# Gated linear attention beside a mixture of experts on one core: another order of the attention's operations, its result copied out a step earlier, 11 groups in place of 12 beside the first unit

## The chip, the cores and the metric

The kernel runs on one core of a Trainium2 chip. The metric is the device time of one execution in microseconds (us), as a median of three runs. TensorE is called PE, VectorE DVE, ScalarE ACT, GpSimd POOL, and SyncE, which only issues transfers here, SP.

## The reference, cut to what matters

A gated linear attention with 4 x 8 heads, 768 tokens and head size 48 gives x, 3072 rows of 384. A mixture of four experts (384 to 1024 to 384, all experts for every row, weighted) and one gated layer (384 to 2048 to 384) follow.

```python
for t in range(S):                                   # attention, for each head
    state = alpha[t][:, None] * state + outer(k[t], v[t])
    y[t] = q[t] @ state
x = y in rows of 384
p = domain_probs / (domain_probs.sum(-1) + 1e-9)
for e in range(4):
    out += p[:, e] * (relu(x @ w1[e]) @ w2[e])
h = out @ w_in
result = (h * clip(h + 3, 0, 6) / 6) @ w_out
```

## The kernel before, in words

**Attention.** The 3072 tokens are twelve units of 256, numbered n = 0 to 11, three for each batch entry. A unit is 7 *groups*, numbered g = 7n + k. Three tables of names give for each k what is emitted: `GROUP[k]` (mostly PE products), `BETWEEN[k]` (copies on ACT, products on DVE) and `CHUNK[k]`, called the *rest* of the group, which is emitted one step later. A name with `-` belongs to the unit before, with `+` to the unit after. The names that matter here:

- `T_tp`, `T_k`, `T_q` are PE transposes of decays, keys and queries, copied out of PSUM by ACT (`tl`, `kt`, `qt`, lines 313 and 334). `tls` multiplies decays on DVE (L342).
- `Sc0` to `Sc3` copy halves of `kt` and `qt` to `kc` and `qc` on ACT (L352). `Su0` to `Su3` then multiply `kt` and `qt` by decays in place on DVE (L362). `C0` to `C3` multiply `kc` by `qc` on PE (L374), `M0` and `M2` mask the result on DVE (L386), `K` turns the keys back (L400, copied by ACT at L408).
- `U` are the state sums on PE (L419), `Z` carries the state through them on DVE (L442, L448), `Y`, `L0` to `L3` and `ST` (the state products, L494) add up the unit's result in PSUM.
- `A` copies that result to SBUF on ACT (L506) and moves it with six transfers into x (L518). `XS` splits x into a high part `xh` (ACT, L802) and a low part `xl` (DVE, L803) and stores x (L805).
- `p0` to `p3`, `r0` to `r2`, `u0`, `u1`, `kk`, `kq`, `tp` prepare the next unit on DVE (L190 to L247). `y0` to `y5` are the value operations of the unit on DVE (L253 to L280).

**Experts.** Each product of the experts is made of three fp32r products: high by high, low by high, high by low. One *step* is a first layer `mm1` of nine products (L829), ACT's ReLU to `hh` (L837), DVE's low part `hl` (L840), and then the second layer `mm2` (L891) of the step before. After `mm1` and `hl` the rest of an earlier group is emitted, after `mm2` a group. Seven of the sixteen 256-column slices of expert weights stay in SBUF while the attention runs, so a block of rows takes 14 steps. Unit 0 and unit 1 are taken alone, with 256 columns (periods 0 and 1); from then on a block is 512 columns and two units. After six such periods the attention is over, and the rest of the experts and the last layer follow. In periods 0 and 1 the product of `mm1` goes to two PSUM tiles by turns; with 512 columns there is one, so the next `mm1` waits until DVE has read the last one for `hl`.

In period 0 the weights, too, are split in a high part (ACT, L779) and a low part (DVE, L781). The probabilities are normalised by four DVE operations (L639 to L643).

**Order.** PE, ACT, DVE and SP run in the order in which the code emits; POOL's is left to a scheduler. The list `ends` says up to which group each period goes: 12 groups (7 to 18) beside the first unit, then 14 in each period. Before period 0 stands a prologue, which runs unit 0 alone, with PE kept busy by idle products (L986).

Of the kernel before, what the change touches and what calls it, by code (L numbers as in the profile page):

```python
# [10 lines left out]
F32 = mybir.dt.float32  # L11
# [7 lines left out]
P = 128  # L19


class Attention:
# [23 lines left out]
    H = 7  # L46

    GROUP = (
        "T_tp -L2 -L3 T_k", "-ST T_q", "C0", "C1", "C2", "C3 K", "U Y L0 L1",
    )  # L50
    BETWEEN = (
        "-X tls", "Sc0 Su0", "Sc1 Su1", "Sc2 M0 Su2", "Sc3 Su3", "M2", "Z0 Z1 Z2 Z3",
    )
    CHUNK = (
        "y0 y1 y2 y3 y4 y5", "-A +p0 +r0", "+p1 +p2 +r1", "-XS +u0", "+u1 +cp +kk +kq", "+tp +p3 +r2", "",
    )

    def __init__(self, ctx, tc, q, k, v, alpha, psum_pool, psum_tag, place, split):
# [232 lines left out]
    def tree(self, n):  # L291
# [53 lines left out]
        def halves(z, l, x):  # L345
            return z.rearrange("p j r (b x w) -> p (j r b) x w", x=2, w=self.W[l])[:, :, x, :]

        def Sc(l):

            for z, out, x, nm in ((s["kt"], s["kc"], 0, "kc"), (s["qt"], s["qc"], 1, "qc")):  # L350
                c = self.wk.tile([P, NP * 2, 64], F32, tag=nm, name=f"{nm}{l}_{n}")
                nc.scalar.copy(c.rearrange("p x (b w) -> p (x b) w", w=self.W[l]), halves(z, l, x))  # L352
                out[l] = c

        def Su(l):

# [146 lines left out]
        def A():  # L503
            ys = wk("ys", [P, NP, U])
            for j in range(2):
                nc.scalar.copy(ys[:, :, P * j : P * j + P], s["py"][j])  # L506
            x = self.place(n)
            parts = (
                (x[0:48, 0:3], ys[0:48, 0:3]),
                (x[48:96, 0:3], ys[64:112, 0:3]),  # L510
                (x[96:128, 0], ys[0:32, 3]),
                (x[96:112, 1], ys[32:48, 3]),
                (x[112:128, 1], ys[64:80, 3]),
                (x[96:128, 2], ys[80:112, 3]),
            )
            for z, (dst, src) in enumerate(parts):
                eng = nc.scalar if n == 0 and z % 2 else nc.sync
                eng.dma_start(dst, src)  # L518

        d = dict(  # L520
            T_tp=T_tp, tls=tls, U=Ust, Y=Y, X=X, ST=ST, A=A,
            XS=lambda: self.split(n),
            T_k=lambda: T(self.kp, "kt"), T_q=lambda: T(self.qp, "qt"),
            M0=lambda: M(0), M2=lambda: M(2), K=K,
        )
        for l in range(4):
            d[f"Sc{l}"] = lambda l=l: Sc(l)
# [35 lines left out]
def tile_gla__then__moe__then__moe2(  # L563
# [458 lines left out]
    load_w(1, 3)  # L1022
    at.load(2, "qka")
    u("p3 r2", 1)
    emit_probs()
    load_p(0)
    load_p(1)


    g = at.H  # L1030
    ends = [3 * at.H - 2, 5 * at.H - 2]
    ends += [ends[1] + 2 * at.H * b for b in range(1, NBLK - 1)]

    todo = []
# [41 lines left out]
    for vi, vv in enumerate(visits):  # L1076
# [16 lines left out]
        for f in range(len(vv["steps"])):  # L1093
            for s_, fn in [x for x in todo if x[0] <= step]:
                todo.remove((s_, fn))
                fn()
            serve()
            low = mm1(vi, f)
            low()
            if rest:  # L1100
                at.rest(rest.pop(0))
            if late:
                next(dec, None)
            pend.append((vi, f))
            done = pend.pop(0) if len(pend) > 1 else None
            if done:
                mm2(*done)
            at_step += 1
            if period < len(ends):
                while g < begun + -(-(ends[period] - begun) * at_step // (2 * S0)):  # L1110
                    if rest:
                        at.rest(rest.pop(0))
                    at.group(g)
                    rest.append(g)
                    g += 1
                if at_step == 2 * S0 and rest:
                    at.rest(rest.pop(0))
            step += 1
            if done is None:
                continue  # L1120

            v2 = visits[done[0]]
            i, z = v2["steps"][done[1]]
            if v2["phase"] > 0 and done[1] == len(v2["steps"]) - 1:
                ended = step
            if done[1] == len(v2["steps"]) - 1 and done[0] + 2 < len(visits):
                after(3, lambda v_=done[0] + 2: load_p(v_))
            if v2["b"] == NBLK - 1 and z == 1:

                if v2["phase"] == 0 and i + S0 + SB < S1:  # L1130
                    get_w(i + S0 + SB)
                elif v2["phase"] == 1 and i - S0 < S2 - S1:
                    for _ in dec:
                        pass
                    get_w(i - S0 + S1)

            if i == (0, S0, S1)[v2["phase"]] + 2 and (v2["phase"] > 0 or v2["b"] == NBLK - 1):
                ph, nb = (v2["phase"], v2["b"] + 1) if v2["b"] + 1 < NBLK else (v2["phase"] + 1, 0)
                if ph <= 2:
                    n = 2 * nb + z  # L1140
                    loads.insert(z, (lambda ph=ph, n=n: load_x(ph, n), lambda ph=ph, n=n: split_x(ph, n)))
                    if ph == 1:
                        if z == 0:
                            load_acc(nb)
                        for e in range(1, EP):
                            loads.append((lambda e=e, n=n: load_acc1(e, n), lambda e=e, n=n: add_acc1(e, n)))
# [32 lines left out]
```

## Time and profile before

| | |
|---|---|
| median of three runs | 1385.18 us (1385.14 to 1385.52) |
| the profiled execution, its time | 1385.72 us |
| its span | 1383.7 us |
| PE busy | 1353.5 us, 98% |
| DVE busy | 843.4 us, 61% |
| ACT busy | 453.1 us, 33% |
| POOL busy | 83.2 us, 6% |
| period 0 | 42.1 to 101.8 us |
| period 1 | 101.8 to 164 us |

The shares are means over stages that differ. The page's 40 slices show DVE at 8 and 9 tenths for the first five slices (35 us each is one slice) and lower later, and PE at 9 from the sixth slice on. Two waits of PE in one list may be of the same cause; what an engine waits for at one place is read in the rows of that place.

### The profile page before, as it was taken

The numbers are of one execution on the slowest core, as the hardware profiler recorded it, in microseconds if no ns is written. First come the engines' busy times: TensorE is split into PE (matmuls) and PEld (weight loads), VectorE is DVE, ScalarE is ACT, GpSimd is POOL, SyncE is SP. The second block draws the span as 40 slices with busy tenths as digits, with TensorE's granted clock in tenths as the row PEclk, the third lists the DMA queues.
The fourth block names the chain that finished last, engine by engine and source line by source line (L and its number), as shares of the span: only waits on it lengthen the run. The fifth ranks groups of instructions, "written<-read, shape, count | busy, mean of one in ns | idle before, by whom it ended". The sixth has DMA issues, their size and how long they took to land.

```text
span 1383.7 us, 26396 instructions
## 1 busy us (share of the span) xinstructions
PE 1353.5 (98%) x10992; PEld 1130.3 (82%) x10992; DVE 843.4 (61%) x1524; ACT 453.1 (33%) x775; POOL 83.2 (6%) x125
## 2 busy tenths in 40 slices
PE   7789899999999999999999999999999999999998
PEld 7788788888888888888888888888888888888898
DVE  8998877777776368657576666645533333334332
ACT  3554444434443143111111111113333333333333
POOL 2000000000000001111112121100000000000000
PEclk9999999999999999999999999999999999999999
DMA  7655543444352276415142423223202020202010
GB/s 196 190 145 144 141 121 102 141 139 124 101 150 72 69 236 215 130 54 163 54 144 62 148 69 106 85 79 120 91 0 46 1 47 0 46 1 46 1 24 23
DMA packets 150279, 132.36 MB, mean 96 GB/s; under 512 B 65680, under 2 KB 130832, under 8 KB 150160
## 3 DMA queue, kind: packets, MB, share of 16 engines
q1 hardware_dynamic: 150016, 130.49, 32.7%
q8 instruction: 86, 1.41, 0.4%
q10 hardware_dynamic: 144, 0.20, 0.1%
q14 instruction: 33, 0.27, 0.1%
HBM read 95.99 MB, written 34.65 MB: 94 GB/s over the span
## 4 chain that ended last, share of the span: by engine, by line
PE 90%; DVE 6%; DMA 1%; ACT 1%; issue 1%; SPq 1%; POOL 0%; DVEq 0%; ACTq 0%; POOLq 0%
PE ph L829 42%; PE po L891 38%; PE po L893 2%; PE py L473 1%; PE py L494 1%; PE pa L374 1%; PE pu L419 1%; PE idle L986 1%; DVE asb L386 1%; DVE qt L362 1%; DVE kt L362 1%; PE pqt L322 0%; PE pkt L322 0%; DVE hl L840 0%; PE py L457 0%
## 5 line engine op out<-in xcount | busy, mean ns | idle before, releaser
L891 PE MATMUL po<-hl,w1h 128*128 128x512 f32 (+1 forms) x858 | 318.0, 380 | 10.1 <-DVE hl L840 10.0
L891 PE MATMUL po<-hh,w1h 128*128 128x512 f32 (+1 forms) x858 | 323.0, 379 | 0.0
L891 PE MATMUL po<-hh,w1l 128*128 128x512 f32 (+1 forms) x858 | 322.7, 379 | 0.0
L837 ACT ACTIVATE hh<-ph 128x512 fp32r<-128x512 f32 (+1 forms) x206 | 117.5, 571 | 500.8 <-PE ph L829 493.7
L840 DVE SCALAR_TENSOR_TENSOR hl<-ph,hh 128x512 fp32r<-128x512 f32 (+1 forms) x206 | 134.4, 652 | 240.6 <-ACT hh L837 240.6
L829 PE MATMUL ph<-xh,w0h 128*128 128x512 f32 (+1 forms) x906 | 255.3, 390 | 3.1 <-ACT xh L802 1.9
L829 PE MATMUL ph<-xh,w0l 128*128 128x512 f32 (+1 forms) x906 | 246.4, 380 | 0.0
L829 PE MATMUL ph<-xl,w0h 128*128 128x512 f32 (+1 forms) x906 | 245.8, 380 | 0.5 <-DVE xl L803 0.4
L829 PEld LDWEIGHTS ph<-xl,w0h 128*128 128x128 f32 x906 | 166.3, 188 | 33.8 <-DVE xl L803 1.1
L829 PEld LDWEIGHTS ph<-xh,w0l 128*128 128x128 f32 x906 | 166.6, 188 | 33.1
L891 PEld LDWEIGHTS po<-hl,w1h 128*128 128x128 f32 x858 | 157.8, 188 | 42.6 <-DVE hl L840 12.1
L829 PEld LDWEIGHTS ph<-xh,w0h 128*128 128x128 f32 x906 | 161.8, 188 | 35.9 <-ACT xh L802 2.2
L891 PEld LDWEIGHTS po<-hh,w1h 128*128 128x128 f32 x858 | 161.4, 188 | 30.8 <-ACT hh L853 0.5
L891 PEld LDWEIGHTS po<-hh,w1l 128*128 128x128 f32 x858 | 161.3, 188 | 30.1
L852 DVE SCALAR_TENSOR_TENSOR g<-g,ph 128x512 f32<-128x512 f32 (+1 forms) x97 | 66.2, 684 | 171.0 <-ACT g L848 171.0
L848 ACT ACTIVATE g<-ph,three 128x512 f32<-128x512 f32 (+1 forms) x97 | 66.2, 684 | 185.0 <-PE ph L829 185.0
L855 DVE SCALAR_TENSOR_TENSOR hl<-g,hh 128x512 fp32r<-128x512 f32 (+1 forms) x97 | 66.6, 687 | 66.6 <-ACT hh L853 66.6
L853 ACT ACTIVATE hh<-g 128x512 fp32r<-128x512 f32 (+1 forms) x97 | 60.9, 629 | 74.6 <-DVE g L852 74.6
L690 POOL TENSOR_TENSOR sq<-hc 128x256 f32<-128x256 f32 x48 | 34.5, 718 | 622.2 <-DVE hc L689 622.2
L934 DVE TENSOR_TENSOR t<-po,pb 128x512 f32<-128x512 f32 (+1 forms) x82 | 52.6, 655 | 0.0
L705 POOL TENSOR_TENSOR a<-a,hc 128x256 f32<-128x256 f32 x48 | 38.8, 808 | 184.6 <-DVE hc L704 184.6
L352 ACT COPY kc<-kt 128x512 f32<-128x512 f32 x48 | 30.3, 632 | 44.6 <-PE pa L374 31.7
(106 smaller groups left out, 1187.1 us busy)
## 6 DMA issues: line engine op xcount, KB each, us to landing
vl<-vd SPq DMA_DIRECT2D x96, 96.0 KB
rx<-x_d SPq DMA_DIRECT2D x24, 384.0 KB
pb<-p_d SPq DMA_DIRECT2D x28, 256.0 KB
raw<-in_moe_w_in_dram SPq DMA_DIRECT2D x24, 256.0 KB
raw<-in_moe_w_out_dram SPq DMA_DIRECT2D x24, 256.0 KB
acc_d<-t SPq DMA_DIRECT2D x20, 256.0 KB
rq<-in_q_dram SPq DMA_DIRECT2D x24, 192.0 KB
rk<-in_k_dram SPq DMA_DIRECT2D x24, 192.0 KB
```

The source lines that it names most:

```text
L352: nc.scalar.copy(c.rearrange("p x (b w) -> p (x b) w", w=self.W[l]), halves(z, l, x))
L690: nc.gpsimd.tensor_tensor(sq, hc, hc, op=mul)
L705: nc.gpsimd.tensor_tensor(a, a, hc, op=add)
L829: pe.matmul(ph[:, 0:n], w[:, j, fs], x[:, j, cs], start=(o == 0 and j == 0), stop=(o == 2 and j == KT - 1),)
L837: nc.scalar.activation(hh[:, 0:n], ph[:, 0:n], AF.Relu)
L840: nc.vector.scalar_tensor_tensor(hl[:, 0:n], ph[:, 0:n], 0.0, hh[:, 0:n].bitcast(F32), op0=ALU.max, op1=sub)
L848: nc.scalar.activation(g[:, c], ph[:, c], AF.Relu, bias=three)
L852: nc.vector.scalar_tensor_tensor(g[:, c], g[:, c], 6.0, ph[:, c], op0=ALU.min, op1=mul)
L853: nc.scalar.activation(hh[:, c], g[:, c], AF.Copy, scale=1.0 / 6.0)
L855: nc.vector.scalar_tensor_tensor(hl[:, c], g[:, c], 1.0 / 6.0, hh[:, c].bitcast(F32), op0=mul, op1=sub)
L891: pe.matmul(accs[vi][m][:, 0:n], w[:, z, ms], h[:, 0:n], **fl)
L934: nc.vector.tensor_tensor(t[:, 0:n], po[:, 0:n], pb, op=mul)
```

## The change

The result of a unit is copied out and moved right behind its state products (`-A` stands in `GROUP[1]`, no longer in the next step's rest). Its transfers go by turns to SP and POOL (for unit 0 to SP, ACT and POOL), where they all went to SP (for unit 0 to SP and ACT). The split of x stands first in the rest of k = 2, no longer in that of k = 3. `y4` moves from the rest of k = 0 to that of k = 1, and `y5` to that of k = 3. The copy `kc` of `Sc0` is made a group earlier, behind `tls`; `qc` stays. Period 0 takes 11 groups (7 to 17), with none added in its steps 3, 6 and 9; every later period begins and ends one group earlier than before. The probabilities are normalised behind the third step of period 0, no longer in the prologue, and their two loads are issued two steps behind that.

```diff
     GROUP = (
-        "T_tp -L2 -L3 T_k", "-ST T_q", "C0", "C1", "C2", "C3 K", "U Y L0 L1",
+        "T_tp -L2 -L3 T_k", "-ST -A T_q", "C0", "C1", "C2", "C3 K", "U Y L0 L1",
     )
     BETWEEN = (
-        "-X tls", "Sc0 Su0", "Sc1 Su1", "Sc2 M0 Su2", "Sc3 Su3", "M2", "Z0 Z1 Z2 Z3",
+        "-X tls Sk0", "Sq0 Su0", "Sc1 Su1", "Sc2 M0 Su2", "Sc3 Su3", "M2", "Z0 Z1 Z2 Z3",
     )
     CHUNK = (
-        "y0 y1 y2 y3 y4 y5", "-A +p0 +r0", "+p1 +p2 +r1", "-XS +u0", "+u1 +cp +kk +kq", "+tp +p3 +r2", "",
+        "y0 y1 y2 y3", "y4 +p0 +r0", "-XS +p1 +p2 +r1", "y5 +u0", "+u1 +cp +kk +kq", "+tp +p3 +r2", "",
     )
...
+        def S1(l, x):
+
+            z, out, nm = (("kt", "kc", "kc"), ("qt", "qc", "qc"))[x]
+            c = self.wk.tile([P, NP * 2, 64], F32, tag=nm, name=f"{nm}{l}_{n}")
+            nc.scalar.copy(c.rearrange("p x (b w) -> p (x b) w", w=self.W[l]), halves(s[z], l, x))
+            s[out][l] = c
...
             for z, (dst, src) in enumerate(parts):
-                eng = nc.scalar if n == 0 and z % 2 else nc.sync
-                eng.dma_start(dst, src)
+                engines = (nc.sync, nc.scalar, nc.gpsimd) if n == 0 else (nc.sync, nc.gpsimd)
+                engines[z % len(engines)].dma_start(dst, src)
...
-            M0=lambda: M(0), M2=lambda: M(2), K=K,
+            M0=lambda: M(0), M2=lambda: M(2), K=K, Sk0=lambda: S1(0, 0), Sq0=lambda: S1(0, 1),
...
     u("p3 r2", 1)
-    emit_probs()
-    load_p(0)
-    load_p(1)
...
-    ends = [3 * at.H - 2, 5 * at.H - 2]
+    ends = [3 * at.H - 3, 5 * at.H - 3]
+    first = [0, 1, 2, 2, 3, 4, 4, 5, 6, 6, 7, 8, 9, 10, 11]
...
-                while g < begun + -(-(ends[period] - begun) * at_step // (2 * S0)):
+                if period == 0 and at_step == 3:
+                    emit_probs()
+                    after(2, lambda: (load_p(0), load_p(1)))
+                while g < begun + (first[at_step] if period == 0 else (ends[period] - begun) * at_step // (2 * S0)):
```

Three places of the new order follow. A name ends with the unit, or with visit and step for `hh`, `hl` and the low weights; the last number counts tiles.

ACT in period 1, around the copy of unit 2's result (`ys`) and the queries of unit 3 (`qt`, `kc0`, `qc0`), before:

```order
L837 ACTIVATE hh_2_3_2009<-ph_2_3_1999 128x256
L334 COPY qt_3_2064<-pqt0_3_2065 128x8x16x4
L334 COPY qt_3_2064<-pqt1_3_2066 128x8x16x4
L352 COPY kc0_3_2085<-kt_3_1968 128x512
L352 COPY qc0_3_2087<-qt_3_2064 128x512
L837 ACTIVATE hh_2_4_2103<-ph_2_4_2093 128x256
L506 COPY ys_2_2107<-py0_2_1845 128x4x128
L506 COPY ys_2_2107<-py1_2_1846 128x4x128
```

and now:

```order
L352 COPY kc0_3_2022<-kt_3_1991 128x512
L842 ACTIVATE hh_2_4_2036<-ph_2_4_2026 128x256
L511 COPY ys_2_2088<-py0_2_1871 128x4x128
L511 COPY ys_2_2088<-py1_2_1872 128x4x128
L334 COPY qt_3_2098<-pqt0_3_2099 128x8x16x4
L334 COPY qt_3_2098<-pqt1_3_2100 128x8x16x4
L352 COPY qc0_3_2119<-qt_3_2098 128x512
L842 ACTIVATE hh_2_5_2133<-ph_2_5_2123 128x256
```

The copies of `ys` went ahead of those of `qt`, and `kc0` ahead of the ReLU of the step.

DVE in period 0, from the low weights behind unit 1's state (`Z`) to those behind unit 2's decays (`tl`), before:

```order
L781 TENSOR_TENSOR w0l_5_1279<-early_l_185,w0h_5_1278 128x768
L840 SCALAR_TENSOR_TENSOR hl_1_0_1293<-ph_1_0_1282,hh_1_0_1292 128x256
L934 TENSOR_TENSOR t_0_0_1302<-po_0_0_812,pb_0_729 128x256
L934 TENSOR_TENSOR t_0_1_1304<-po_0_0_812,pb_0_729 128x256
L934 TENSOR_TENSOR pb_0_729<-po_0_1_813,pb_0_729 128x256
L342 TENSOR_TENSOR tl1_2_1371<-tl0_2_1310 128x128
L342 TENSOR_TENSOR tl2_2_1373<-tl1_2_1371 128x64
L342 TENSOR_TENSOR tl3_2_1375<-tl2_2_1373 128x32
L342 TENSOR_TENSOR tl4_2_1377<-tl3_2_1375 128x16
L781 TENSOR_TENSOR w1l_5_1380<-early_h_184,w1h_5_1379 128x768
```

and now:

```order
L786 TENSOR_TENSOR w0l_6_1340<-early_h_184,w0h_6_1339 128x768
L845 SCALAR_TENSOR_TENSOR hl_1_2_1357<-ph_1_2_1346,hh_1_2_1356 128x256
L342 TENSOR_TENSOR tl1_2_1430<-tl0_2_1369 128x128
L342 TENSOR_TENSOR tl2_2_1432<-tl1_2_1430 128x64
L342 TENSOR_TENSOR tl3_2_1434<-tl2_2_1432 128x32
L342 TENSOR_TENSOR tl4_2_1436<-tl3_2_1434 128x16
L786 TENSOR_TENSOR w1l_6_1441<-early_l_185,w1h_6_1440 128x768
```

The three weighted sums of the first visit (`t`, `pb`), which stood here, now come ahead of `Z`; the place itself lies two steps later in the period.

DVE at the end of period 1, from the last `hl` with 256 columns to the first with 512, before:

```order
L840 SCALAR_TENSOR_TENSOR hl_3_5_2805<-ph_3_5_2794,hh_3_5_2804 128x256
L803 TENSOR_TENSOR xl_0_1_2234<-rx_0_3_2683,xh_0_1_2233 128x3x256
L200 TENSOR_TENSOR rq5_2366<-rq5_2366,ra5_2372 128x8x48
L362 TENSOR_TENSOR kt_4_2548<-kt_4_2548,tl3_4_2575 128x16x32
L362 TENSOR_TENSOR qt_4_2639<-qt_4_2639,tl3_4_2575 128x16x32
L203 TENSOR_TENSOR rk5_2369<-rk5_2369,ra5_2372 128x8x48
L205 TENSOR_TENSOR t1_5_2846<-ra5_2372 128x384
L216 TENSOR_TENSOR kp_111<-rk5_2369,t1_5_2846 128x2x2x48 x2
L216 TENSOR_TENSOR qp_110<-rq5_2366,t1_5_2846 128x2x2x48 x2
L840 SCALAR_TENSOR_TENSOR hl_4_0_2867<-ph_4_0_2856,hh_4_0_2866 128x512
```

and now:

```order
L845 SCALAR_TENSOR_TENSOR hl_3_5_2773<-ph_3_5_2762,hh_3_5_2772 128x256
L808 TENSOR_TENSOR xl_0_1_2202<-rx_0_3_2664,xh_0_1_2201 128x3x256
L193 TENSOR_TENSOR rq5_2394<-rq5_2394,ra5_2400 128x768
L197 TENSOR_TENSOR w1_5_2780<-rq5_2394,rk5_2397 128x384
L247 TENSOR_REDUCE dg1_5_2782<-w1_5_2780 128x8
L391 TENSOR_TENSOR asb0_4_2813<-pa00_4_2738,mask_123 128x512
L391 TENSOR_TENSOR asb0_4_2813<-pa01_4_2739,mask_123 128x512
L367 TENSOR_TENSOR kt_4_2574<-kt_4_2574,tl2_4_2599 128x32x16
L367 TENSOR_TENSOR qt_4_2671<-qt_4_2671,tl2_4_2599 128x32x16
L280 TENSOR_TENSOR y8_112<-y8_112,pr1_4_2625 128x2x2x48 x2
L200 TENSOR_TENSOR rq5_2394<-rq5_2394,ra5_2400 128x8x48
L845 SCALAR_TENSOR_TENSOR hl_4_0_2832<-ph_4_0_2821,hh_4_0_2831 128x512
```

`Su3` (the `kt` and `qt` with `tl3`) and the operations of `u1`, `kk` and `kq` (L203 to L216) left the stretch ahead of the first `hl` with 512 columns; the split of x now has more DVE work behind it.

## Rows read from the trace of the kernel before

**Rows 1.** Busy time by stretch: stretch, length, PE, PEld, DVE, ACT, POOL, clock, DMA, GB/s.

```profile
42.10:104.20 62.10, 51.04 (x834) 45.75 (x834) 59.55 (x115) 34.40 (x64) 0.00 (x0) 0.97 0.64 176
104.20:170.70 66.50, 58.53 (x1191) 52.95 (x1191) 57.63 (x123) 33.01 (x71) 0.00 (x0) 1.00 0.50 139
170.70:470.00 299.30, 299.27 (x4255) 242.03 (x4256) 214.84 (x408) 121.02 (x226) 0.00 (x0) 1.00 0.41 117
```

**Rows 2.** Waits of PE, 44 to 104 us: total, times, longest.

```profile
PE po L891 <- DVE hl L840: 8.4, 6, 2.4
```

**Rows 3.** Waits of DVE, 104 to 171 us.

```profile
DVE hl L840 <- ACT hh L837: 4.8, 2, 2.5
DVE kt L362 <- ACT kc L352: 1.3, 2, 0.8
```

**Rows 4.** DVE timeline, end of period 1: start, duration, operation, [idle before <- releaser].

```profile
166.55 0.68 DVE L362 TENSOR_TENSOR kt<-kt,tl 128x512 f32<-128x512 f32 x1
...
169.98 0.69 DVE L840 SCALAR_TENSOR_TENSOR hl<-ph,hh 128x512 fp32r<-128x512 f32 x1
```

**Rows 5.** PE timeline at the first step with 512 columns.

```profile
168.19 0.69 PE L374 MATMUL pa<-qc,kc 48*64 48x64 f32 x32
168.82 0.71 PE L400 MATMUL pk<-ident,kt 64*128 64x64 f32 x16
170.72 0.96 PE L829 MATMUL ph<-xh,w0h 128*128 128x512 f32 x3 [1.20 <-DVE hl L840]
```

**Rows 6.** DVE and ACT timeline, first two steps of period 0.

```profile
45.75 0.24 DVE L639 TENSOR_REDUCE probs<-probs 128x24 f32<-128x96 f32 x1
...
46.81 0.41 DVE L840 SCALAR_TENSOR_TENSOR hl<-ph,hh 128x256 fp32r<-128x256 f32 x1
...
48.04 0.95 DVE L781 TENSOR_TENSOR w1l<-early_h,w1h 128x768 fp32r<-128x768 f32 x1
...
46.52 0.86 ACT L779 CAST w1h<-early_h 128x768 fp32r<-128x768 f32 x1
```

**Rows 7.** DVE timeline behind unit 1's state, period 0.

```profile
81.04 0.74 DVE L934 TENSOR_TENSOR t<-po,pb 128x256 f32<-128x256 f32 x2
...
82.23 0.98 DVE L342 TENSOR_TENSOR tl<-tl 128x128 f32<-128x128 f32 x4
84.35 0.96 DVE L781 TENSOR_TENSOR w1l<-early_h,w1h 128x768 fp32r<-128x768 f32 x1 [1.15 <-ACT w1h L779]
```

**Rows 8.** DVE timeline, value operations of unit 3 and what follows.

```profile
121.98 0.56 DVE L274 TENSOR_TENSOR pr<-pr 128x384 f32<-128x384 f32 x1
122.58 0.63 DVE L280 TENSOR_TENSOR y<-y,pr 128x192 f32<-128x192 f32 x2
123.72 0.69 DVE L362 TENSOR_TENSOR kt<-kt,tl 128x512 f32<-128x512 f32 x1 [0.51 <-ACT kc L352]
```

**Rows 9.** ACT timeline at the same place.

```profile
123.02 0.67 ACT L352 COPY kc<-kt 128x512 f32<-128x512 f32 x1
123.56 0.62 ACT L352 COPY qc<-qt 128x512 f32<-128x512 f32 x1
...
124.35 1.09 ACT L506 COPY ys<-py 128x512 f32<-128x512 f32 x2
```

**Rows 10.** PE timeline, longest wait in period 0, and clock of the stretch behind it.

```profile
65.93 0.62 PE L891 MATMUL po<-hl,w1h 128*128 128x256 f32 x3 [2.42 <-DVE hl L840]
...
66.00:70.00 4.00, 4.00 (x58) 0.57 0.52 139
```

**Rows 11.** SP and ACT timelines: transfers of x and the split that waits.

```profile
36.98 2.25 SPq L518 DMA_DIRECT2D rx<-ys  x3
91.61 4.50 SPq L518 DMA_DIRECT2D rx<-ys  x6
...
41.21 0.83 ACT L802 CAST xh<-rx 128x768 fp32r<-128x768 f32 x1
97.64 0.83 ACT L802 CAST xh<-rx 128x768 fp32r<-128x768 f32 x1 [1.36 <-DMA rx<-ys]
```

More of the change, by code (lines that the diff above doesn't have):

```diff
@@ L346, in halves @@
             return z.rearrange("p j r (b x w) -> p (j r b) x w", x=2, w=self.W[l])[:, :, x, :]
+        def S1(l, x):
[3 more added lines that the diff above has]
+            s[out][l] = c
         def Sc(l):
[L350 to L353, printed above, removed]
+            for x in range(2):
+                S1(l, x)
         def Su(l):
```

## The prediction

> **What bounds the kernel now.** I read first the busy time by stretch [rows 1]. From 170.7 to 470 us PE is busy 299.27 of 299.30 us, so a change of order inside that stretch can only cost. What can be won lies ahead of it: PE stands 62.10 - 51.04 = 11.1 us in period 0 and 66.50 - 58.53 = 8.0 us in period 1. In period 0 DVE is busy 59.55 of 62.10 us, and the list of PE's waits shows why PE stands: 8.4 us in six waits for `hl`, which comes late because DVE runs its queue in order [rows 2]. Period 0 is DVE's.
>
> Period 1 is a loop of two halves. DVE's own waits there are few [rows 3]: 4.8 us for `hh` and 1.3 us for `kc`, all around `ST` and `T_q` of units 3 and 4. From `Su0` of a unit to `Z`, DVE does not stand at all and PE waits for it; from `Z` through `T_k`, `ST` and `T_q` DVE waits for PE and ACT. So the time to the end of period 1 is DVE's work plus DVE's standing, and I count the change on DVE up to the `hl` that begins at 169.98 us [rows 4]. There PE has one PSUM tile: its next `mm1` waits 1.20 us for that `hl` and begins at 170.72 us [rows 5]. From there on only PE's remaining work counts.
>
> **The change part by part, on DVE up to that `hl`.**
>
> *One group less.* Through both periods 25 groups are emitted in place of 26, with their rests. What leaves is `Su3` and `u1`, `kk`, `kq` of the last group: 169.98 - 166.55 = 3.43 us [rows 4]. `y4`, `y5` and the split only change places.
>
> *Probabilities.* Their four operations take 46.81 - 45.75 = 1.06 us [rows 6] and come back two steps later, so no work is saved. The first `hl` comes 1.06 us sooner, but the low weights behind it need ACT's cast, which began at 46.52 us and now stands behind `kc0` (123.56 - 123.02 = 0.54 us [rows 9]): it ends at 46.52 + 0.86 + 0.54 = 47.92, where DVE arrives at 48.04 - 1.06 = 46.98. DVE stands 0.9 us that it did not.
>
> *The new gaps.* No group is added in steps 3, 6 and 9, which lets DVE catch up there, but groups 13 to 15, which are heavy on PE, then come in steps 10 to 12 without a pause. Before, DVE had the weighted sums of the first visit (82.23 - 81.04 = 1.19 us) between `Z` and the low weights, and still stood 1.15 us for the cast [rows 7]. Now these sums come ahead of `Z`, and the cast stands behind `kc0`: DVE stands 1.15 + 1.19 + 0.54 = 2.9 us, 1.7 more.
>
> *Value operations, and the sums behind the state products.* `y4` and `y5` took 0.56 + 0.63 = 1.2 us [rows 8] in the half in which DVE waits: behind them it still stood 0.51 us for `kc`. They now lie behind `Su0`, in the half in which DVE sets the time. Against that, `kc0` is gone from between `qt` and `qc0` (0.54 us), while the copies of the sums (1.09 us [rows 9]) stand ahead of those of `qt` and are mostly covered by `T_q`'s 16 transposes (one set of 16 takes 0.71 us [rows 5]): `qc0` comes 0.54 - 0.4 = 0.15 us sooner, and the `qt` half of `Su0`, which no longer comes behind a waiting `kt` half, starts another 0.25 us sooner. Net for a unit 1.2 - 0.4 = +0.8 us; in period 1 this happens for units 3 and 4: +1.6 us. (For unit 2 it is inside the 2.9 us.)
>
> *The split a group sooner, and two queues.* One of these splits waited 1.36 us for its transfers, but on ACT [rows 11], while DVE had work; the split on DVE is where the time is set, and it only changes its place. Issue of six transfers takes SP 4.50 us [rows 11]; three of them now go to POOL. No transfer of POOL stands in the trace. From below: three as fast as SP's three, 2.25 us of issue, which hides. From above: as slow as six on SP, from 91.61 until the split at 97.64, 6.0 us. The split stays about two steps behind the copies (those two times are 6.0 us apart already), and DVE reaches it with work in hand, so both ends cost nothing there. In the prologue the split begins 41.21 - 36.98 = 4.2 us behind the first issue, right behind ACT's copies for the next unit; up to 6.0 - 4.2 = 1.8 us could show. I take 0, as the nearest row has half the transfers on a queue and these are a third, and keep 1.8 for the range. The Trainium skill ("DMA: Bandwidth & Descriptors", section on latency and other measured facts) gives about 1 us to the first byte of a transfer from POOL and 0.6 us from SP or ACT; by that the estimate is 0.4 us a transfer, hidden as well. No run here shows it yet.
>
> *Sum.* -3.43 + 0.9 + 1.7 + 1.6 = +0.8 us at the `hl`: the work saved is lost again in standing. Then PE: in the run before, `C3` and `K` of group 33 were already done ahead of the `mm1` at 170.72 us; now they are still to come, two groups of products [rows 5]: 0.63 us from start to start and 0.71 us, 1.3 us. As PE has no idle time behind [rows 1], this is added in full: +2.1 us. On the profiled execution's 1385.72 us that is 1387.8; the median of the runs lies 0.54 us lower, so I forecast 1387.3 us. About 0.2%, 2.8 us, is what a measurement of this kernel can tell from no change: this is inside it.
>
> In the later blocks the split now shares a step with `M0`, `Su2`, `p1`, `p2` and `r1`, the fullest of the seven steps on DVE. Over a unit DVE has room there (214.84 of 299.30 us busy [rows 1]), so I cost it at nothing; if one `hl` came 0.5 us late in each of the eight units left, that would be 4 us at most.
>
> **Rivals.**
>
> *The moved group is won in full.* DVE's standing does not grow: the waits for `hh` and `kc` [rows 3] shrink since copies come earlier, the gaps fall where DVE was behind. Then -3.43 + 1.3 = -2.1 us; with the 0.4 us for each of units 2 to 4 as well, -3.3 us: 1381.9 to 1383.1. For it speaks that DVE was busy 96% of period 0, and that PE stood 11 us there; against it that the same standing comes back at named places above. Only the lower half of this case is a difference that can be told.
>
> *The clock falls at the start of the blocks of 512 columns.* PE must stand there until the `hl` at about 170.8 us, as before, and has `C3` and `K` less to do ahead of it: 1.20 + 1.3 = 2.5 us [rows 5], and more by what the split comes sooner. In period 0, behind a wait of 2.42 us and shorter ones, the granted clock was 0.57 for 4.0 us [rows 10], thus mostly at the lower of the two levels: 4.0 x 0.43 = 1.7 us lost. There DVE's lag covered it; here nothing does, as PE is the bound from that point: 1387.3 + 1.7 = 1389.0 us. It decides from a wait about as long as that of 2.42 us. The page "TensorE: Matmul & The Clock Gate" of the Trainium skill (section on HAM oscillation) says in my words that a PE which stands waiting for data falls back to the lower clock and pays for it anew each time; rows 10 agree, with 0.57, and by that rule the forecast would be this case. Against it: the 2.5 us are a difference of two long sums, and in period 0 other waits of the six [rows 2] lay close ahead of the long one.
>
> *POOL's transfers come late.* They would hold the first split in the prologue, and everything behind it: 1387.3 + 1.8 = 1389.1 us, and more from 6.0 us on, when every unit's split waits too. It decides from 4.2 us behind the copies.
>
> *The change does not do what it says*, in that the group that leaves period 0 is caught up in period 1: excluded by the order, period 1 has 14 groups before and now.
>
> **How the numbers follow.** Forecast 0.45, its own range 1385.5 to 1388.5; won in full 0.24; clock 0.23; POOL or the steps of the split late 0.08. Faster by over 0.2% (under 1382.4): half of the second and a little of the forecast, 0.15. Slower (over 1387.95): the last two and a fifth of the others' upper ends, 0.35. Within: 0.50. The range holds the second case's middle and the third with its spread: 1382.4 to 1390.0.
>
> **What would show it.** In the profile after: the first `hl` with 512 columns at about 170.8 us, with a longer wait of PE ahead of the second `mm1` of that size; DVE standing near 2.9 us for the last cast in period 0 and near 0.9 us for the first; DVE waiting for `hh` more than before in period 1; `ptt` waiting on `Z`'s last sum in step 11. If that `hl` comes at 169 us or sooner, the second case holds and my standing is wrong; if a granted clock under 1 appears between 170 and 178 us, the third; if PE stands anywhere from 180 to 460 us, the steps of the split are too full. The prediction is wrong if the time is under 1384 or over 1389.5.

## The result, and the profile after

The changed kernel took 1396.11 us (median of 6 runs, 1394.81 to 1400.48), the kernel before 1385.37 us beside it (6 runs, 1385.14 to 1386.21). The ratio is 1.0081, with a 95% interval of 1.0067 to 1.0095: 9.3 to 13.2 us slower. The profiled execution is the fastest of the six: it took 1394.81 us, with a span of 1393.1 us, 9.4 us longer than before. So the rows below explain these 9.4 us and not the whole 10.7 us between the medians.

Busy time by stretch of the changed kernel, in the columns of [rows 1]:

```profile
42.10:104.20 62.10, 51.63 (x804) 47.31 (x805) 54.27 (x104) 34.95 (x64) 1.51 (x3) 0.94 0.64 175
104.20:170.70 66.50, 60.73 (x1175) 55.07 (x1173) 56.02 (x119) 31.95 (x64) 2.97 (x6) 0.93 0.49 140
170.70:470.00 299.30, 293.58 (x4074) 236.85 (x4075) 216.89 (x416) 126.33 (x229) 10.41 (x21) 0.99 0.40 117
```

DVE is less busy in the first two stretches, as the change wanted, and PE is not done sooner: its clock is 0.94 and 0.93 where it was 0.97 and 1.00 (what that costs where DVE sets much of the time shows in experiment 4), and it stands 299.30 - 293.58 = 5.7 us behind 170.7 us where it stood 0.03.

PE's waits of the changed kernel from 44 to 500 us, then DVE's from 44 us to the first `hl` with 512 columns (total, times, longest), beside [rows 2, 3]:

```profile
PE po L896 <- DVE hl L845: 6.9, 3, 2.7
PE ph L834 <- DVE hl L845: 6.0, 4, 3.4
PE po L896 <- DVE t L939: 4.3, 2, 2.8
```

```profile
DVE hl L845 <- ACT hh L842: 6.4, 2, 3.2
DVE w1l L786 <- ACT w1h L784: 4.7, 2, 3.6
DVE tl L342 <- ACT tl L313: 2.5, 3, 1.0
DVE qt L367 <- ACT qc L352: 1.0, 2, 0.7
DVE sc L453 <- PE pu L424: 0.6, 1, 0.6
DVE w0l L786 <- ACT w0h L784: 0.4, 1, 0.4
```

Of the 6.0 us in which PE's first layer waits for `hl`, one wait of 3.40 us opens the blocks of 512 columns, and three of 0.86 us open the three periods behind. The place is the end of a period. DVE's timeline there, beside [rows 4]:

```profile
166.45 0.42 DVE L845 SCALAR_TENSOR_TENSOR hl<-ph,hh 128x256 fp32r<-128x256 f32 x1
166.78 0.95 DVE L808 TENSOR_TENSOR xl<-rx,xh 128x768 fp32r<-128x768 f32 x1
...
169.69 1.28 DVE L391 TENSOR_TENSOR asb<-pa,mask 128x512 f32<-128x512 f32 x2
170.89 0.68 DVE L367 TENSOR_TENSOR kt<-kt,tl 128x512 f32<-128x512 f32 x1
171.49 0.68 DVE L367 TENSOR_TENSOR qt<-qt,tl 128x512 f32<-128x512 f32 x1
172.09 0.62 DVE L280 TENSOR_TENSOR y<-y,pr 128x192 f32<-128x192 f32 x2
172.63 0.55 DVE L200 TENSOR_TENSOR rq<-rq,ra 128x384 f32<-128x384 f32 x1
173.10 0.68 DVE L845 SCALAR_TENSOR_TENSOR hl<-ph,hh 128x512 fp32r<-128x512 f32 x1
```

The `hl` begins at 173.10 us, not at 169.98. From the split's low part to it DVE has 6.32 us of work, all in two rests and a group of the same step. PE's timeline, beside [rows 5], and then, beside [rows 10], the busy row of the stretch behind with its clock:

```profile
173.83 0.98 PE L834 MATMUL ph<-xh,w0h 128*128 128x512 f32 x3 [3.40 <-DVE hl L845]
174.65 1.36 PE L834 MATMUL ph<-xh,w0l 128*128 128x512 f32 x3
175.81 1.48 PE L834 MATMUL ph<-xl,w0h 128*128 128x512 f32 x3
```

```profile
174.00:178.00 4.00, 4.00 (x12) 3.06 (x13) 2.11 (x6) 0.60 (x1) 0.00 (x0) 0.60 0.36 121
```

Three such products take 0.85 and 0.84 us at the full clock in the second and third set (experiment 6's rows below); here they take 1.36 and 1.48. The clock of 0.60 over 4 us is mostly the lower of the two levels (1.2 and 2.4 GHz). From this `mm1` to the next group's products PE needs 5.95 us (173.83 to 179.78), before 4.31 (170.72 to 175.03): 1.64 us.

### The profile page after: what moved, and what is told of

Same layout as the page of the kernel before. It is cut to its first block, busy times and chain, and to the rows that moved or that the text cites. A ratio compares the mean times of both kernels' runs of the same rounds, so it can differ in the third digit from the quotient of the medians.

```text
span 1393.1 us, 26467 instructions
## 1 busy us (share of the span) xinstructions
PE 1359.3 (98%) x10992; PEld 1135.8 (82%) x10992; DVE 841.4 (60%) x1524; ACT 459.3 (33%) x775; POOL 101.2 (7%) x160
## 4 chain that ended last, share of the span: by engine, by line
PE 90%; DVE 6%; ACT 1%; DMA 1%; issue 1%; SPq 0%; POOL 0%; DVEq 0%; ACTq 0%; POOLq 0%
PE ph L834 41%; PE po L896 38%; PE po L898 2%; PE py L478 2%; PE py L499 2%; PE pa L379 1%; DMA rx<-ys 1%; PE pu L424 1%; DVE qt L367 1%; PE idle L991 1%; DVE asb L391 1%; DVE hl L845 1%; PE pk L405 1%; DVE kt L367 1%; PE py L462 1%
## 5 line engine op out<-in xcount | busy, mean ns | idle before, releaser
L858 ACT ACTIVATE hh<-g 128x512 fp32r<-128x512 f32 (+1 forms) x97 | 60.9, 629 | 74.6 <-DVE g L857 74.6
L523 POOL DMA_DIRECT2D rx<-ys x35 | 17.5, 507 | 460.0 <-ACT ys L511 203.3
```

The source lines that it names most:

```text
L858: nc.scalar.activation(hh[:, c], g[:, c], AF.Copy, scale=1.0 / 6.0)
```

## The experiments

Numbers are those that the expectations use. A ratio is to the kernel before, which ran beside each. Theory 1: the end of a period is too full on DVE, because of the split's new place. Theory 2: the new order inside a group makes DVE stand. Theory 3: POOL's transfers are late. Theory 4, later: the gaps. Theory 5, later: a group less in period 0 only turns into standing.

| | median us | ratio (95%) |
|---|---|---|
| changed | 1396.11 | 1.0081 (1.0067 to 1.0095) |
| 1 no rest at a period's end | 1391.69 | 1.0040 (1.0027 to 1.0054) |
| 2 split in k = 3, 12 groups | 1389.11 | 1.0021 (1.0012 to 1.0030) |
| 3 order in a group back | 1393.04 | 1.0053 (1.0040 to 1.0066) |
| 4 no POOL | 1398.73 | 1.0085 (1.0070 to 1.0099) |
| 5 = 1 with p1 sooner | 1391.58 | 1.0043 (1.0030 to 1.0055) |
| 6 PE kept busy in the wait | 1396.05 | 1.0073 (1.0060 to 1.0085) |
| 7 = 1 and 3 | 1392.57 | 1.0047 (1.0033 to 1.0060) |
| 8 = 2 and 3 | 1386.36 | 1.0004 (0.9995 to 1.0013) |
| 9 before, no rest at a period's end | 1384.22 | 0.9991 (0.9982 to 1.0000) |
| 10 even gaps | 1397.02 | 1.0078 (1.0065 to 1.0091) |
| 11 = 8 with the split in k = 2 | 1389.00 | 1.0019 (1.0009 to 1.0028) |
| 12 = 8, no rest at a period's end | 1385.24 | 0.9996 (0.9988 to 1.0005) |
| 13 = 11, 11 groups in period 0 alone | 1392.50 | 1.0047 (1.0034 to 1.0060) |
| 14 = 12, probabilities in the prologue | 1385.37 | 1.0000 (0.9991 to 1.0009) |
| 15 = 9, 13 groups in period 0 | 1386.34 | 1.0004 (0.9995 to 1.0012) |

**Experiment 1.**

```diff
-                if at_step == 2 * S0 and rest:
-                    at.rest(rest.pop(0))
```

> The changed kernel, but the last rest of a period (y5, u0: 173.10 - 172.09 = 1.0 us of DVE) is not emitted at the period's end; it goes into the next step. Theory 1 (the period's end is too full on DVE: between the low part of the split and the first 512-column hl stand 6.32 us of work where there were 4.76): the first 512-column hl comes 1.0 us sooner, PE's wait there falls from 3.40 to about 2.4 us, and the three waits of 0.86 us at the ends of later periods go: 1.0 + 2.6 = 3.6 us less, up to 5 if the clock stays up: 1391 to 1392.5 us. Theory 2 (the reordered copies and value operations make DVE stand) and theory 3 (POOL's transfers): the 1.0 us only, no less than 1395 us.

4.4 us less, inside theory 1's range, but not by all of its steps. No wait of PE is left from 190 to 500 us, which is 2.6 us, and the clock stays up behind the first wait, now 2.39 us, which is 1.6 us more. The 1.0 us at the first `hl` with 512 columns did not come: it begins 127.3 us behind the first `hl` of all, in the changed kernel 127.2.

**Experiment 2.**

```diff
-        "y0 y1 y2 y3", "y4 +p0 +r0", "-XS +p1 +p2 +r1", "y5 +u0", ...
+        "y0 y1 y2 y3", "y4 +p0 +r0", "+p1 +p2 +r1", "-XS y5 +u0", ...
...
-    ends = [3 * at.H - 3, 5 * at.H - 3]
+    ends = [3 * at.H - 2, 5 * at.H - 2]
...
-                while g < begun + (first[at_step] if period == 0 else ...):
+                while g < begun + -(-(ends[period] - begun) * at_step // (2 * S0)):
```

> The changed kernel with the split back in the rest of k = 3 and 12 groups (7 to 18) in period 0, evenly spread, every later period one group later again; the order inside a group (A, kc0, y4, y5), POOL's transfers and the probabilities stay as changed. Theory 1: the period's end is as in the kernel before, no granted clock under 1 behind 170 us, no wait of PE from 180 to 480 us: 1386 to 1389 us. Theory 2: the standing of DVE stays, 1392 us or more. Theory 3: 1395 us or more.

7.0 us less, 1389.11 us, just over the upper edge of theory 1. The later periods are clean, but the clock fell all the same behind a wait of only 1.73 us. PE's timeline there, and the busy row behind it:

```profile
172.67 1.51 PE L834 MATMUL ph<-xh,w0h 128*128 128x512 f32 x3 [1.73 <-DVE hl L845]
```

```profile
174.00:176.00 2.00, 2.00 (x6) 1.62 (x5) 1.00 (x2) 0.00 (x0) 0.00 (x0) 0.50 0.04 8
```

**Experiment 3.**

```diff
-        "-X tls Sk0", "Sq0 Su0", ...
+        "-X tls", "Sc0 Su0", ...
-        "y0 y1 y2 y3", "y4 +p0 +r0", "-XS +p1 +p2 +r1", "y5 +u0", ...
+        "y0 y1 y2 y3 y4 y5", "+p0 +r0", "-XS +p1 +p2 +r1", "+u0", ...
```

> The changed kernel with kc0 back behind the queries, and y4 and y5 back in the rest of k = 0; the split, the 11 groups and POOL's transfers stay as changed. Theory 1: DVE has y5 (0.6 us) less ahead of the first 512-column hl, and stands as before around the copies: 1394 to 1396 us. Theory 2: DVE's standing for hh and for the last w1h cast goes down by 2.6 us or more, and the time with it: 1392 us or less. Theory 3: no change.

3.1 us less: more than theory 1 allowed, a little less than theory 2 asked. Both costs are there: DVE's stands for `hh` and `w1h` fall by 2.5 us together (6.4 to 5.3 and 4.7 to 3.3), and the three waits of PE at the later period ends fall from 0.86 to 0.3 us each, as `y5` no longer stands there.

**Experiment 4.**

```diff
-                engines = (nc.sync, nc.scalar, nc.gpsimd) if n == 0 else (nc.sync, nc.gpsimd)
+                engines = (nc.sync, nc.scalar) if n == 0 else (nc.sync,)
```

> The changed kernel with the transfers of x on SP alone (unit 0: SP and ACT), as in the kernel before. Theories 1 and 2: within 1 us of 1396, as no split waits long for them now. Theory 3 (POOL's transfers are late, or their issue disturbs DVE): 4 us or more less, 1392 us or less; the waits of the split for its transfers go.

Theory 3 falls: without POOL nothing is won. The median of 1398.73 us lies 2.6 us over that of the changed kernel, where theories 1 and 2 allowed 1, but the ratios 1.0085 and 1.0081 are not told apart. POOL's transfers in the changed kernel, and SP's of the same unit:

```profile
93.94 1.51 POOL L523 DMA_DIRECT2D rx<-ys  x3 [55.27 <-ACT ys L511]
```

```profile
93.67 2.05 SPq L523 DMA_DIRECT2D rx<-ys  x3
```

Three are issued in 1.51 us, no slower than SP's three in 2.05 us [rows 11: six in 4.50]; the trace has POOL's 2.8 to 3.6 us from issue to landing.

This run's trace also shows what the clock costs in period 0. In the changed kernel and here PE stands the same 2.75 us for the same `t`. PE's timeline there, the busy row behind, and DVE's wait for the state sums (`pu`), of the changed kernel and then of experiment 4:

```profile
80.21 0.36 PE L896 MATMUL po<-hh,w1h 128*128 128x256 f32 x1 [2.75 <-DVE t L939]
80.00:84.00 4.00, 3.79 (x145) 3.56 (x149) 3.14 (x9) 0.00 (x0) 0.00 (x0) 1.00 0.89 271
82.64 0.35 DVE L453 TENSOR_TENSOR sc<-sd,pu 128x192 f32<-128x192 f32 x1 [0.58 <-PE pu L424]
```

```profile
80.15 0.55 PE L896 MATMUL po<-hh,w1h 128*128 128x256 f32 x1 [2.75 <-DVE t L939]
80.00:84.00 4.00, 3.85 (x73) 3.66 (x73) 1.90 (x5) 0.00 (x0) 0.00 (x0) 0.50 0.89 278
84.35 0.35 DVE L453 TENSOR_TENSOR sc<-sd,pu 128x192 f32<-128x192 f32 x1 [2.35 <-PE pu L424]
```

The clock stayed up in one execution and fell to the lower level in the other, and DVE stood 2.35 - 0.58 = 1.8 us more. It is not the missing POOL: experiments 1 and 6, with POOL, show 0.58, experiments 5 and 7, with POOL too, 2.35.

**Experiment 6.** A try at the clock alone.

```diff
+                if period == 2 and at_step == 1:
+                    spare = ps3.tile([P, 512], F32, tag="ps3", name="spare")
+                    for j in range(24):
+                        pe.matmul(spare[:, 0:U], wts[(0, 1)][0][:, 0, 0:P], xs[(0, 0)][0][:, 0, 0:U], start=True, stop=True)
```

> The changed kernel with 24 products of 128 x 256 into a spare PSUM tile, put where PE stands 3.40 us for the first 512-column hl (estimate 24 x 0.12 = 2.9 us, within the wait; nothing reads the tile). If the lower clock behind that wait costs time (the first step behind it took 5.95 us, against 4.31 in the kernel before), the granted clock stays 1.0 from 170 to 180 us and 1.6 us go: about 1394.5 us. If the clock is no cost, or falls for another reason, no change: 1396.

PE's timeline in its profile, and the busy row behind the wait:

```profile
170.22 3.14 PE L1127 MATMUL spare<-xh,w0h 128*128 128x256 f32 x24
173.69 0.96 PE L834 MATMUL ph<-xh,w0h 128*128 128x512 f32 x3 [0.34 <-DVE hl L845]
174.49 0.85 PE L834 MATMUL ph<-xh,w0l 128*128 128x512 f32 x3
175.19 0.84 PE L834 MATMUL ph<-xl,w0h 128*128 128x512 f32 x3
```

```profile
174.00:178.00 4.00, 4.00 (x19) 3.01 (x17) 3.23 (x7) 0.71 (x2) 0.00 (x0) 1.00 0.36 120
```

The products start at the same time as in the changed kernel (173.69 and 173.83), the clock is 1.00, and the next `mm1` starts at 179.27, not 181.05: 1.78 - 0.14 = 1.64 us saved in the profiled execution, as the arithmetic above had it. The timed runs do not show it: the ratios 1.0073 and 1.0081 have overlapping intervals. So the price is shown in one profile each and not in the median.

**Experiment 7.** Both diffs of 1 and 3.

> Experiments 1 and 3 together: no rest at a period's end, and kc0, y4 and y5 in their old places; the split, the 11 groups, POOL and the probabilities stay as changed. If the period's end and the order inside a group are two separate costs, their gains add: 1396.1 - 4.4 - 3.1 = 1388.6 us. If they are one cost seen twice (the order back takes y5 out of the period's end too), 1390 to 1391.7 us.

1392.57 us, 0.9 us over the range of the second reading: the gains do not add. With `y5` out of the period's end by the old order, leaving the last rest out is worth nothing that can be told (1.0053 and 1.0047). Part of this is one cost seen twice: of the 2.6 us at the later period ends the old order had already won 1.6 (experiment 3). Part is the clock: in this profile it fell behind a wait of 2.40 us, where in experiment 1 it stayed up behind 2.39 (rows in the last section), and the step behind took 5.93 us, not 4.30; and DVE stood 1.8 us more than in experiment 1 for the state sums, as in experiment 4. How much of the missing 4 us is the one and how much the other is not shown.

**Experiment 8.** Both diffs of 2 and 3.

> Experiment 2 with kc0, y4 and y5 back in their old places: of the change only A behind the state products, POOL's transfers and the later probabilities are left. Theory 2 (the order of the copies and value operations costs 1.5 to 3 us): 1386 to 1387.6 us. If that order costs nothing beside the split's place: 1389 us as in experiment 2; then the probabilities or A cost the 3.4 us that experiment 2 stands above the kernel before.

1386.36 us, theory 2's reading. With `A` early, POOL and the later probabilities alone the kernel is where it was; they cost nothing that can be told. The order costs 1.0021 - 1.0004 = 0.0017, 2.4 us, with 12 groups. In the two profiles 1.6 us lie in the clock: the first step with 512 columns takes 5.89 us in experiment 2, 4.30 here, where PE does not wait ahead of it.

**Experiment 11.** The split alone, on top of 8.

```diff
-        "y0 y1 y2 y3 y4 y5", "+p0 +r0", "+p1 +p2 +r1", "-XS +u0", ...
+        "y0 y1 y2 y3 y4 y5", "+p0 +r0", "-XS +p1 +p2 +r1", "+u0", ...
```

> Experiment 8 (12 groups, kc0, y4 and y5 in their old places) with the split of x first in the rest of k = 2, as in the change; the last group of a period is k = 4 again, so the split does not stand at the period's end. Theory 1, narrow (the cost is that the full step of the split stands at the period's end): within 1.5 us of experiment 8, 1386 to 1388 us, no wait of PE from 180 to 480 us. Theory 1, wide (the split beside M0, Su2, p1, p2 and r1 costs wherever it stands): PE waits 2 us or more for hl behind each split of periods 0 and 1, and the time is 1389 us or more.

1389.00 us, at the lower edge of the wide reading, though with no wait of PE from 190 to 500 us, as the narrow one had it. Against experiment 8 it is 0.0015, 2.1 us, about as much as the uncertainty of such a difference; the profiles agree: the `mm1` behind the first `hl` with 512 columns starts 126.8 us after the first `hl` of all, in experiment 8 after 124.8. PE's waits from 42 to 190 us, of experiment 8 and then of 11:

```profile
PE po L896 <- DVE hl L845: 7.4, 6, 2.0
```

```profile
PE po L896 <- DVE hl L845: 11.1, 7, 2.4
PE ph L834 <- DVE hl L845: 2.1, 1, 2.1
```

So the split beside `M0`, `Su2`, `p1`, `p2` and `r1` costs in periods 0 and 1 wherever the period ends.

**Experiment 5.** Experiment 1 with one line changed.

```diff
-        "y0 y1 y2 y3", "y4 +p0 +r0", "-XS +p1 +p2 +r1", ...
+        "y0 y1 y2 y3", "y4 +p0 +r0 +p1", "-XS +p2 +r1", ...
```

> Experiment 1 (no rest at the period's end) with p1 (0.95 us of DVE) moved from the step of the split to the step before. Theory 1: the first 512-column hl comes 0.9 us sooner against the split, PE's wait there falls from 2.4 to about 1.5 us, and PE's waits behind the splits of periods 0 and 1 fall by as much: 1389.5 to 1391 us. If the step of the split does not set the time: 1391.7 us, as experiment 1.

1391.58 us, no change. In its profile (1394.34 us, the slowest of the five runs) PE's waits for `hl` fell, from 6.8 to 4.8 us and from 2.4 to 1.4, but that for the split's low part rose from 2.2 to 3.9 and that for `hh` from 1.0 to 3.2: the 0.95 us only moved ahead of the split.

**Experiment 10.**

```diff
-                while g < begun + (first[at_step] if period == 0 else (ends[period] - begun) * at_step // (2 * S0)):
+                while g < begun + (ends[period] - begun) * at_step // (2 * S0):
```

> The changed kernel with its 11 groups of period 0 spread evenly over the 14 steps, without the gaps in steps 3, 6 and 9. Theory 4 (the gaps make PE stand early, and the groups 13 to 15 behind them keep PE so full that DVE then stands 3.63 us for the last w1h cast): that wait falls below 1.5 us, period 0 (from its first hl to the first hl of period 1, 62.2 us in the changed kernel, 59.4 before) falls to 60 us or less, the whole to about 1394 us. If 11 groups cost that time however they are spread: period 0 stays at 62 us, the whole at 1396.

Theory 4 falls. DVE's waits of this run from 44 to 171 us:

```profile
DVE w1l L786 <- ACT w1h L784: 4.8, 1, 4.8
DVE w0l L786 <- ACT w0h L784: 2.5, 1, 2.5
```

The stand for the last cast grew instead, to 4.8 us, period 0 took 64.0 us in this profile, and the whole 1397.02.

**Experiment 13.** Experiment 11 with one line changed.

```diff
-    ends = [3 * at.H - 2, 5 * at.H - 2]
+    ends = [3 * at.H - 3, 5 * at.H - 2]
```

> Experiment 11 (split in k = 2, order of kc0, y4, y5 as before) with 11 groups in period 0 and 15 in period 1, so that all later periods are as in experiment 11 (1389.0 us). If a group less in period 0 turns into standing of DVE (theory 5): from its first hl to the first hl of period 1 it takes 61.5 us or more, as with 12 groups, period 1 takes the group's 3.4 us more, and the time is 2 to 4 us above experiment 11: 1391 to 1393 us. If the cost of 11 groups lies at the later period ends and in the group still owed: period 0 is 2 to 3 us shorter than in experiment 11 and period 1 as much longer, 1388.5 to 1389.5 us.

The total is theory 5's (1392.50), its course only half. Starts of the first `hl` of periods 0, 1 and 2 in the DVE timelines give these lengths (each is rounded for itself):

| | period 0 | period 1 | both |
|---|---|---|---|
| before | 59.4 | 63.7 | 123.2 |
| changed | 62.2 | 65.0 | 127.2 |
| 3 | 62.9 | 63.4 | 126.3 |
| 8 | 60.9 | 62.9 | 123.9 |
| 11 | 61.7 | 64.4 | 126.1 |
| 13 | 60.1 | 68.9 | 129.0 |
| 9 | 59.4 | 60.8 | 120.3 |
| 15 | 64.0 | 60.3 | 124.2 |

From 11 to 13 one group goes from period 0 to period 1: period 0 becomes 1.6 us shorter, not 3.4, and period 1 becomes 4.5 us longer. Experiment 3, with 25 groups, takes as long over both as 11 with 26: the 3.4 us of DVE work that left bought nothing there. Each row is one execution, and the clock's chance alone can be worth 1.8 us in period 0 (experiment 4).

**Experiments 9, 12, 14 and 15.** Tries for a faster version: the kernel before without the last rest (the diff of 1); experiment 8 the same way; this with the probabilities and their loads back in the prologue; and experiment 9 with `ends = [3 * at.H - 1, 5 * at.H - 2]`.

> The kernel before, without the last rest at a period's end (u1, kk, kq: 169.98 - 167.76 = 2.2 us of DVE go into the next step). Theory 1: the first 512-column hl comes up to 0.9 us sooner (not before its hh, which begins at 169.36 and takes 0.59), PE's wait of 1.20 us shrinks to about 0.5: 1385 us, or up to 1 us later if the work that moved is missed in the next step.

> Experiment 8 without the last rest at a period's end, as experiment 9 is the kernel before without it: a try for a version faster than both. DVE has u1, kk and kq (2.2 us) less ahead of the first 512-column hl, but PE had no wait there in experiment 8: 1384 to 1386.5 us.

> Experiment 12 with the probabilities and their loads back in the prologue: the kernel before without the last rest, with A behind the state products and POOL's transfers. If the later probabilities cost by DVE's first stand (1.1 us): 1384 to 1385 us. If they cost nothing: 1385.2 us as experiment 12.

> Experiment 9 (the kernel before without the last rest at a period's end) with 13 groups in period 0 and 13 in period 1; later periods as in experiment 9 (1384.2 us). Theory 5 (the number of groups in period 0 sets how DVE's work and its waiting half fall against the steps): period 0 need not grow by the group's 3.4 us, period 1 falls by more than period 0 grows: 1382.5 to 1384 us. If DVE's work alone counts: period 0 3 us longer, period 1 3 us shorter, 1384 to 1385 us.

Experiment 9 is the fastest kernel of the study, 1.5 us under the kernel before by the medians, with an interval (0.9982 to 1.0000) that just touches no change: so the period's end was probably worth something already there, as its profile has it: the `mm1` behind the first `hl` with 512 columns starts 121.9 us after the first `hl` of all, in the kernel before after 123.9. 12 and 14 are not told from the kernel before. 15 came out over both of its readings: a group more cost period 0 4.6 us and saved period 1 only 0.5. Taking a group out of a period saved 0.5 to 1.6 us in these two pairs of profiles, and putting one in cost 4.5 to 4.6; the medians went up by 3.5 us (13 against 11) and 2.1 us (15 against 9).

## Why the prediction was wrong

It forecast 1387.3 us, at most 1390.0, with no change as the likeliest. The result is 9 us over the forecast. In the two profiled executions its steps stand so:

| step | forecast | measured, us |
|---|---|---|
| a group less on DVE | -3.43 | 110.89 busy from 44 us to the `hl`, before 114.56: -3.67 |
| first `hl` sooner | -1.06 | 45.87 - 46.81 = -0.94 |
| stand for the first low weights | +0.9 | 1.10 |
| stand for the last cast | 2.9 (+1.7) | 3.63 (+2.5) |
| units 3 and 4 | +1.6 | `hh` 6.4 - 4.8, copies 1.0 - 1.3: +1.3 |
| stands not in the sum | 0 | `tl` 2.5 - 1.2, `sc` 0.6, `w0l` 0.4: +2.3 |
| first `hl` with 512 columns | +0.8 | 173.10 - 169.98 = +3.12 |
| the two groups of products PE still owes | +1.3 | +1.5 (experiments 1 and 5, below) |
| clock at the first 512-column step | 0 (a rival's +1.7) | +1.64 |
| later periods | 0, at most 4 | 3 x 0.86 = +2.6 |

DVE's two waits for low weights, beside [rows 6, 7]:

```profile
48.28 0.96 DVE L786 TENSOR_TENSOR w1l<-early_h,w1h 128x768 fp32r<-128x768 f32 x1 [1.10 <-ACT w1h L784]
...
92.20 0.96 DVE L786 TENSOR_TENSOR w1l<-early_l,w1h 128x768 fp32r<-128x768 f32 x1 [3.63 <-ACT w1h L784]
```

**The steps that failed.** First, "In the later blocks the split now shares a step with `M0`, `Su2`, `p1`, `p2` and `r1` ... I cost it at nothing". The room was taken as a mean over a unit, but with 11 groups the end of a period puts that step, the next rest (`y5`, `u0`) and a new block's first `hl` behind each other, where PE has one PSUM tile. That is 2.6 us in the later periods, gone in experiment 1. With 12 groups the split in the same place brings no such wait (experiment 11), but costs 2.1 us in periods 0 and 1, which the sum had as "it only changes its place". Second, and as costly, the term for DVE's standing: it was counted at the places where the trace of before already showed a wait. It grew 18.2 - 11.4 = 6.8 us over all, not 4.2, so the first `hl` with 512 columns came 3.12 us later and not 0.8: `tl` waits longer, and `sc` and `w0l` wait where nothing waited. (These 2.6 us and the 2.1 of the split's place lie in the same stretch and are not to be added; the 0.25 us by which `Su0`'s `qt` half was to start sooner is worked out from no row.) Third, the clock was set up as a rival of the forecast, though both could happen, and did; its price was right (1.7 against 1.64). Its condition was not: it was set at a wait of some 2.4 us, here the wait was 3.40, as the `hl` came late, and experiments 1, 2 and 7 show that the length does not decide.

The sum from the trace: 3.12 + 1.64 + 2.6 = 7.3 of the 9.4 us. The owed products can be read from experiments 1 and 5, where PE no longer waits, and the clock stays up, from the `mm1` behind the first `hl` with 512 columns on: from its start to the end of the span both take 1214.7 us, while the kernel before and experiments 8, 9 and 11 to 15, all with 26 groups and the clock up, take 1213.0 to 1213.2. That is 1.5 us, and 8.8 of the 9.4 us in all; 0.6 are not named.

**What was right.** Of the signs named, the growing waits for `hh` and for the two casts came, and so did the two that spoke for rivals: a clock under 1 between 170 and 178 us, and PE standing behind 180 us. Two did not: the `hl` at 170.8 us, and PE's transposes of decays waiting for `Z` (one such wait of 1.1 us stood in period 1 before and is gone; DVE waits for their copies instead). The work saved is lost in standing; the named stands lie where they were put, within 0.8 us; POOL costs nothing that can be told (experiment 4), and neither do `A` early and the probabilities (experiments 8 and 14). As a ladder of ratios: 8 stands at 1.0004, the split's place adds 0.0015 (11), 11 groups 0.0034 (3), the order inside the group with 11 groups 0.0028 (changed). Each step has an uncertainty of about 0.0015, so the first is just at the edge of it; the step of 11 groups holds the gaps, too, and the split at the later period ends, as no run has 11 groups with the split in k = 3.

**What stays open.** What decides whether the clock falls. It goes with the spread: of the changed kernel's six timed runs the four of 1394.8 to 1396.4 us had a mean granted clock of 0.993, the one of 1397.85 us 0.992 and the one of 1400.48 us 0.990; of experiment 4's five the two of 1395.3 us had 0.993, the three of 1398.7 to 1400.2 us 0.990 and 0.989. The kernel before, beside the experiments, kept within 3.6 us (1384.8 to 1388.4). Of the 0.0034 for 11 groups, 4.7 us, the trace of experiment 3 names 4.1: 1.5 of owed products, 1.6 of the clock (its first step with 512 columns takes 5.93 us, not 4.31), and 1.0 in three waits of PE of 0.3 us.

## What to carry to other kernels

Where DVE works beside PE in turns, a queue's work and its standing are one account: taking work out where it waits anyway, or moving it into the half that it sets, gained less than the work here, and adding cost more in two pairs of profiles. Before moving an operation, list what stands in the queue between the moved one and the next operation that PE needs at each border of a stage, not the mean load of the stage. And a clock that falls behind a wait is no alternative to a late result but comes on top of it.

## What the runs showed of the hardware

The length of the wait does not decide whether PE's clock falls. It fell behind 3.40 us in the changed kernel and behind 1.73 us in experiment 2 (rows above), and behind 2.40 us in experiment 7, while in experiment 1 it stayed up behind 2.39 us. PE's timeline and the busy row of experiment 1, then of 7:

```profile
175.31 0.96 PE L834 MATMUL ph<-xh,w0h 128*128 128x512 f32 x3 [2.39 <-DVE hl L845]
176.11 0.85 PE L834 MATMUL ph<-xh,w0l 128*128 128x512 f32 x3
176.80 0.84 PE L834 MATMUL ph<-xl,w0h 128*128 128x512 f32 x3
174.00:178.00 4.00, 2.69 (x12) 2.24 (x13) 3.90 (x11) 1.48 (x3) 0.00 (x0) 1.00 0.29 101
```

```profile
175.73 0.96 PE L834 MATMUL ph<-xh,w0h 128*128 128x512 f32 x3 [2.40 <-DVE hl L845]
176.53 1.18 PE L834 MATMUL ph<-xh,w0l 128*128 128x512 f32 x3
177.50 1.48 PE L834 MATMUL ph<-xl,w0h 128*128 128x512 f32 x3
176.00:180.00 4.00, 4.00 (x12) 3.11 (x12) 2.78 (x7) 0.60 (x1) 0.00 (x0) 0.61 0.39 132
```

Nor does it fall each time behind the same wait: behind 2.75 us in period 0 it stayed at 1.00 in the changed kernel and fell to 0.50 in experiment 4. What PE did before the wait sets these cases apart only in part: in experiment 2 it had stood 2.33 us for `xl` until 167.63, five us before; in experiment 1 it had stood 0.54 us there and in experiment 7 only 0.16.

The page "TensorE: Matmul & The Clock Gate" of the Trainium skill (section on HAM oscillation) describes a PE that falls back each time that it stands for a transfer, with waits longer than those of 1.73 to 2.75 us here. Of our waits only that of 3.40 us is of its kind, and the trace agrees there (clock 0.60 behind it); the prediction read it as a rule for every stand, and for the shorter ones the traces show a risk and not a rule.

The transfers of x in the prologue land at different times in executions whose instructions are the same up to there, with and without POOL. ACT's first split of experiment 9 (SP and ACT issue), and of experiment 1 (POOL too); in the kernel before it did not wait [rows 11], in the changed one 0.61 us:

```profile
42.88 0.83 ACT L802 CAST xh<-rx 128x768 fp32r<-128x768 f32 x1 [1.48 <-DMA rx<-ys]
```

```profile
42.77 0.83 ACT L807 CAST xh<-rx 128x768 fp32r<-128x768 f32 x1 [2.42 <-DMA rx<-ys]
```

So 1 to 2 us of a profiled execution's length are this chance, and lengths between the first `hl`s compare better than the span.
